# Queueing the preparation of the next token block behind its step's last operations, in a two-layer MoE kernel

## The chip, the cores and the metric

The kernel runs on one core of a Trainium2 chip. Its metric is device time in microseconds; before the change the median of three runs is 1727.81 us (1726.5 to 1728.76). All engines named here belong to the one core: PE (TensorE matmul), PEld (its weight loads), DVE (VectorE), ACT (ScalarE), POOL (GpSimd) and SP (SyncE, which issues the DMAs).

## What is computed

The reference applies two softmax attentions through 32 packed queries, and then two dense layers to the 4608 tokens of width 512. The change lies in the second of them:

```
def _moe2_ref(x, w_gate, w_val, w_out):
    g = x @ w_gate
    silu = g * (1.0 / (1.0 + np.exp(-g)))
    val = x @ w_val
    return (silu * val @ w_out)

# attention (8 x 8 heads x 576 x 64) -> x (4608 x 512)
# x = _moe_ref(x)    d_ff 2048, leaky max
# x = _moe2_ref(x)   d_ff 1536
```

## The kernel before the change

**Layer two.** `NBLK` = 6 blocks s of 768 tokens, each as two halves of 384 columns (`T`). A block takes `NF2` = 12 steps f of 128 hidden columns; step n = 12 s + f is one call of `gv_step` (L1186), and 72 of them follow the 256 units of layer one. A step multiplies the gate and value matrices by seven products (`PRODUCTS`: A11, S2, A12, S3, S1, A22, S4) in place of eight; each of them reads sums of pieces of the token block. One product is six matmuls of 384 columns, since each factor is split into a high and a low part (`mm3`, L302, whose matmuls have the lines L305 to L307). Products 0, 2, 4 and 6 go to one pair of PSUM banks (named xb, and vb for the second of a step), 1, 3 and 5 to the other (yb). Product 2 adds to the bank of product 0, so it can start only when ACT has copied that bank (L1204); product 3 adds to the bank of product 1, so it can start only when DVE has read it in `add(u2, yb, p1)` (an L1184 instruction). Between the products stand the output units of the step before (`out_unit`, tile o), three matmuls of 512 columns each, whose weights are the high and low parts ph and pl that `halves` (L1241) makes on ACT and POOL.

**The order of the work on PE** is written out: each product waits in the queue behind the one before (`behind`, `tc.issue_after`). On DVE, ACT and POOL the instructions of a step stand in the order that a scheduler gives them: it takes what is ready by its own timeline, and earlier program text goes first where two are ready.

**The preparation of a token block** (`prepare_x`, L1124): `load` (DMA of the eight raw tiles xr, L1069), `A11` (high part on ACT, L1120, low part on DVE, L1121, two tiles each), `S` (`sums_x`: L1088 twice on DVE, L1089 twice on POOL), `S2` (L1111 twice on DVE, then L1120 and L1121 twice each), `A12` (L1120, L1121 twice each) and `D4` (`last_sum`, L1095 twice on DVE). The other four splits (S3, S1, A22, S4) are called inside step f = 11 by `next_x` (L1198). `NEXT_X` (L94) names the step of block s in which the program text prepares block s + 1: load 3, A11 and S 6, S2 7, A12 8, D4 9. The split parts lie in a ring of 40 pieces of 384 columns (`fifth`, L1099), of which a block takes 28, so the first three products of the next block have room beside the whole of the present one.

Below, "boundary" means the steps f = 10, 11 and the following f = 0, 1, and "boundary 1 to 2" the one between the blocks 1 and 2.

Of the kernel before, what the change touches and what calls it, by code (L numbers as in the profile page):

```python
# [11 lines left out]
AF = mybir.ActivationFunctionType  # L12
ALU = mybir.AluOpType
# [80 lines left out]
NEXT_X = dict(load=3, A11=6, S=6, S2=7, A12=8, D4=9)  # L94
# [10 lines left out]
def f32(ap):  # L105
    return ap.bitcast(F32)
# [3 lines left out]
def tile_kernel(  # L110
# [23 lines left out]
    nc = tc.nc  # L134
# [671 lines left out]
    for f in range(NF1):  # L806
# [11 lines left out]
        d=quad(3, ["h", "at"]),  # L818
# [64 lines left out]
    for b in range(2, B):  # L883
        d0 = 2 * NB1 * (b - 1)
        steps_of = attention(b)
        for entry in STEPS.split():
            d, names = entry.split(":")
# [172 lines left out]
    def load_x(s):  # L1060
        for t in range(2):
            for c in range(KC):
                raw = utile("u", [P, T], f"xr{s}_{t}{c}")
                raw2[s, t, c] = raw
                a0 = t0 = (2 * s + t) * T
                while t0 < a0 + T:
                    j, c0 = divmod(t0, HS)
                    n = min(HS - c0, a0 + T - t0)
                    nc.sync.dma_start(  # L1069
                        out=raw[:, t0 - a0 : t0 - a0 + n], in_=x1d[j][:, c, c0 : c0 + n]  # L1070
                    )
                    t0 += n
# [6 lines left out]
    def sums_x(s):  # L1079

        if s:
            raw2[s, "S1"] = [utile("x", [P, T], f"xs1_{s}{e}") for e in range(2)]
        else:
            s1 = vp.tile([P, 2, T], F32, tag="v", name="xs1_0")
            raw2[s, "S1"] = [s1[:, e] for e in range(2)]
        for e in range(2):
            a11, a21, a22 = (raws_of(s, n)[e] for n in ("A11", "A21", "A22"))
            nc.vector.tensor_tensor(out=raw2[s, "S1"][e], in0=a21, in1=a22, op=ALU.add)  # L1088
            nc.gpsimd.tensor_tensor(out=a21, in0=a11, in1=a21, op=ALU.subtract)  # L1089

    def last_sum(s):

        for e in range(2):
            a12, s2 = raws_of(s, "A12")[e], raws_of(s, "A11")[e]
            nc.vector.tensor_tensor(out=a12, in0=a12, in1=s2, op=ALU.subtract)  # L1095
# [10 lines left out]
    def split_x(s, name):  # L1106

        if name == "S2":
            src = raws_of(s, "A11")
            for e in range(2):  # L1110
                nc.vector.tensor_tensor(  # L1111
                    out=src[e], in0=raw2[s, "S1"][e], in1=src[e], op=ALU.subtract
                )
        else:
            at = dict(S3="A21", S4="A12").get(name, name)
            src = raw2[s, "S1"] if name == "S1" else raws_of(s, at)
        n = 4 * (len(PRODUCTS) * s + PRODUCTS.index(name))
        x = [[fifth(n + 2 * e + i) for e in range(2)] for i in range(2)]
        for e in range(2):
            nc.scalar.activation(out=x[0][e], in_=src[e], func=AF.Copy)  # L1120
            nc.vector.tensor_tensor(out=x[1][e], in0=src[e], in1=f32(x[0][e]), op=ALU.subtract)  # L1121
        xs2[s, name] = x

    def prepare_x(s, name):  # L1124
        if name == "load":
            load_x(s)
        elif name == "S":
            sums_x(s)
        elif name == "D4":
            last_sum(s)  # L1130
        else:
            split_x(s, name)
# [5 lines left out]
    def load_gv(n):  # L1138
        if n >= NBLK * NF2:
            return  # L1140
        f = n % NF2
        gvw[n] = [
            wpool.tile([P, 7, 2 * P], F32R, tag="C", name=f"gv{n}_{t}", bufs=WBUFS["C"])
            for t in range(2)
        ]
        for t in range(2):
            nc.sync.dma_start(out=f32(gvw[n][t]), in_=wgvd[f][:, t])
# [17 lines left out]
    def product(bank, n, k, start):  # L1165

        s = n // NF2
        x = xs2[s, PRODUCTS[k]]
        hi, lo = gvw[n]
        with behind():  # L1170
            for e in range(2):
                c = slice(e * P, (e + 1) * P)
                last = mm3(
                    bank,
                    (hi[:, k, c], lo[:, k, c]),
                    (x[0][e], x[1][e]),
                    start and e == 0,
                    e == 1,
                    skip_group_check=True,
                )  # L1180
        before[:] = [last]

    def add(out, bank, x):
        nc.vector.tensor_tensor(out=out, in0=bank, in1=x, op=ALU.add)  # L1184

    def gv_step(n, between):  # L1186

        s, f = divmod(n, NF2)  # L1190
        p1, u2, u3, s1, s2 = (
            gp2.tile([P, T], F32, tag=t, name=f"{t}_{n}", bufs=b)
            for t, b in (("p1", 2), ("u2", 2), ("u3", 2), ("s1", 1), ("s2", 1))
        )
        def bank(tag, name):
            return ps.tile([P, 512], F32, tag=tag, name=f"{name}{n}", bufs=2)[:, :T]

        def next_x(name):  # L1198
            if f == NF2 - 1 and s + 1 < NBLK:
                split_x(s + 1, name)  # L1200

        xb, yb = bank("h", "xb"), bank("at", "yb")
        product(xb, n, 0, True)
        nc.scalar.activation(out=p1, in_=xb, func=AF.Copy)  # L1204
        product(yb, n, 1, True)
        add(u2, yb, p1)
        between(0)
        product(xb, n, 2, False)
        nc.scalar.activation(out=s1, in_=xb, func=AF.Sigmoid)
        nc.vector.tensor_tensor(out=s1, in0=xb, in1=s1, op=ALU.mult)  # L1210
        next_x("S3")
        product(yb, n, 3, False)
        add(u3, yb, p1)
        between(1)
        between(2)
        xb = bank("h", "vb")
        product(xb, n, 4, True)
        add(u3, xb, u3)
        next_x("S1")
        product(yb, n, 5, False)  # L1220
        add(p1, yb, p1)
        nc.scalar.activation(out=s2, in_=p1, func=AF.Sigmoid)  # L1222
        nc.gpsimd.tensor_tensor(out=s2, in0=s2, in1=p1, op=ALU.mult)  # L1223
        between(3)
        product(xb, n, 6, False)
        add(u2, xb, u2)
        nc.vector.tensor_tensor(out=s1, in0=s1, in1=u2, op=ALU.mult)  # L1227
        halves(n, 0, s1)
        nc.gpsimd.tensor_tensor(out=s2, in0=s2, in1=u3, op=ALU.mult)
        halves(n, 1, s2)  # L1230
        between(4)
        next_x("A22")
        between(5)
        next_x("S4")
        load_gv(n + 2)
        if s + 1 < NBLK:
            for name, d in NEXT_X.items():
                if f == d:
                    prepare_x(s + 1, name)

    def halves(n, t, x):  # L1241
        hi = utile("a", [P, T], f"ph{n}_{t}", F32R)
        nc.scalar.activation(out=hi, in_=x, func=AF.Copy)  # L1243
        lo = utile("a", [P, T], f"pl{n}_{t}", F32R)
        nc.gpsimd.tensor_tensor(out=lo, in0=x, in1=f32(hi), op=ALU.subtract)  # L1245
        ps2[n, t] = hi, lo
# [70 lines left out]
    for n in range(NBLK * NF2):  # L1317
        gv_step(n, lambda i, n=n: out_next(n, i))
# [39 lines left out]
```

## Time and profile before

| | |
|---|---|
| median of three runs | 1727.81 us (1726.5 to 1728.76) |
| the profiled execution | 1725.98 us, of which the span of the trace is 1723.9 us |
| PE busy | 1623.3 us, 94% of the span |
| PEld / DVE / POOL / ACT busy | 1462.9 / 928.5 / 801.2 / 682.7 us |
| mean granted TensorE clock | 0.973 |
| layer two in the trace | from 860.51 us to the end |

The share of a busy engine is an average over both layers. In layer two PE is busy without a break through most steps, and the breaks stand in a few places; so what counts is the length of single steps, read from the start of the first matmul of a product, and what ended a wait of PE. Matmuls overlap: a matmul's own time (0.33 us) is longer than its distance to the next (0.17 us).

### The profile page before, as it was taken

How to read it: one execution, taken by the hardware profiler on the slowest of the kernel's cores; microseconds unless marked ns; L12 is line 12 of the kernel's file. 1: busy time of each engine (PE TensorE's matmuls, PEld its weight loads, DVE VectorE, ACT ScalarE, POOL GpSimd, SP SyncE). 2: the span in 40 equal slices, each digit the busy share in tenths (PEclk: the TensorE clock that was granted, in tenths of full speed). 3: DMA queues.
4: the chain of work that ended last, by engine and by line, in shares of the span. 5: the costliest groups of instructions: out<-in, count | busy, mean ns of one | idle time of the engine just before them, and what ended most of it. 6: DMA issues, size and time to landing. Idle time of an engine off the chain costs nothing.

```text
span 1723.9 us, 28559 instructions
## 1 busy us (share of the span) xinstructions
PE 1623.3 (94%) x10708; PEld 1462.9 (85%) x10708; DVE 928.5 (54%) x1621; ACT 682.7 (40%) x1511; POOL 801.2 (46%) x824
## 2 busy tenths in 40 slices
PE   6698999999999899999999999989989999999997
PEld 3467798988888789889999989979989998998997
DVE  6988757555756546565653453363364345335332
ACT  5775645555554445554521322232232232223222
POOL 3557744655554555547543343333333343343332
PEclk7799999999999999999999999999999999999999
DMA  9433464636444452543664564455355445444442
GB/s 232 121 101 113 118 160 115 159 108 149 124 123 119 133 151 71 139 143 124 221 247 149 186 197 161 171 183 189 144 187 173 168 179 184 171 169 170 168 171 80
DMA packets 227370, 266.11 MB, mean 154 GB/s; under 512 B 130464, under 2 KB 189856, under 8 KB 227232
## 3 DMA queue, kind: packets, MB, share of 16 engines
q1 hardware_dynamic: 227232, 264.30, 48.8%
q8 instruction: 84, 1.38, 0.3%
q14 instruction: 54, 0.44, 0.1%
HBM read 214.70 MB, written 49.55 MB: 153 GB/s over the span
## 4 chain that ended last, share of the span: by engine, by line
PE 68%; DMA 9%; DVE 8%; issue 5%; POOL 4%; ACT 4%; SPq 2%; POOLq 0%; ACTq 0%; DVEq 0%
PE o L306 5%; PE o L307 5%; PE o L305 5%; PE acc L1029 5%; PE acc L1030 4%; PE acc L1035 4%; PE yb L305 4%; PE yb L307 4%; PE yb L306 4%; DMA wgvd<-cva 4%; PE vb L306 3%; PE vb L307 3%; PE vb L305 3%; PE h L305 3%; PE xb L306 3%
## 5 line engine op out<-in xcount | busy, mean ns | idle before, releaser
L1016 POOL TENSOR_TENSOR lo<-g,hi 128x288 fp32r<-128x288 f32 x256 | 227.3, 889 | 237.7 <-ACT hi L1014 195.1
L1223 POOL TENSOR_TENSOR s<-s,p 128x384 f32<-128x384 f32 x72 | 73.9, 1027 | 463.1 <-ACT s L1222 463.1
L1006 DVE SCALAR_TENSOR_TENSOR g<-h,sg,m 128x288 f32<-128x288 f32 x256 | 130.2, 509 | 162.8 <-ACT m L1003 131.3
L305 PE MATMUL h<-a2h,ppw 128*128 128x288 f32 x512 | 163.0, 318 | 22.7 <-DVE g L1006 16.9
L1184 DVE TENSOR_TENSOR u<-vb,u 128x384 f32<-128x384 f32 x144 | 80.2, 557 | 185.8 <-PE vb L307 185.3
L1014 ACT ACTIVATE hi<-g 128x288 fp32r<-128x288 f32 x256 | 113.1, 442 | 153.1 <-DVE g L1006 146.0
L307 PE MATMUL o<-wp,ph 128*128 128x512 f32 x432 | 172.0, 398 | 0.0
L306 PE MATMUL o<-wp,ph 128*128 128x512 f32 x432 | 171.6, 397 | 0.0
L305 PE MATMUL o<-wp,pl 128*128 128x512 f32 x432 | 168.9, 391 | 1.0 <-POOL pl L1245 1.0
L1245 POOL TENSOR_TENSOR pl<-s,ph 128x384 fp32r<-128x384 f32 x144 | 146.8, 1040 | 29.9 <-ACT ph L1243 29.9
L307 PE MATMUL h<-a2l,ppw 128*128 128x288 f32 x512 | 153.1, 299 | 0.0
L305 PE MATMUL yb<-ring,gv 128*128 128x384 f32 x432 | 146.3, 339 | 7.1 <-DVE u L1184 6.8
L306 PE MATMUL h<-a2h,ppw 128*128 128x288 f32 x512 | 152.8, 298 | 0.0
L1222 ACT ACTIVATE s<-p 128x384 f32<-128x384 f32 x72 | 37.8, 525 | 288.2 <-DVE p L1184 288.2
L1184 DVE TENSOR_TENSOR u<-yb,p 128x384 f32<-128x384 f32 x144 | 79.4, 551 | 130.9 <-PE yb L307 129.5
L305 PEld LDWEIGHTS h<-a2h,ppw 128*128 128x128 f32 x512 | 98.2, 192 | 56.9 <-DVE g L1006 27.1
L307 PE MATMUL yb<-ring,gv 128*128 128x384 f32 x432 | 144.9, 335 | 0.0
L306 PE MATMUL yb<-ring,gv 128*128 128x384 f32 x432 | 144.8, 335 | 0.0
L1003 ACT ACTIVATE m<-h,sal 128x288 f32<-128x288 f32 x256 | 125.5, 492 | 42.1 <-PE h L307 41.0
L1243 ACT ACTIVATE ph<-s 128x384 fp32r<-128x384 f32 x144 | 73.4, 523 | 150.7 <-DVE s L1227 136.4
L305 PE MATMUL xb<-ring,gv 128*128 128x384 f32 x288 | 97.3, 338 | 7.9 <-DVE u L1184 7.7
L307 PEld LDWEIGHTS h<-a2l,ppw 128*128 128x128 f32 x512 | 98.1, 192 | 0.8 <-issue 0.8
(234 smaller groups left out, 4364.9 us busy)
## 6 DMA issues: line engine op xcount, KB each, us to landing
gv<-wgvd SPq DMA_DIRECT2D x144, 896.0 KB, 6.2
wgvd<-cva SPq DMA_DIRECT2D x84, 256.0 KB, 2.5
cva<-in_moe_w_out_dram SPq DMA_DIRECT2D x28, 512.0 KB, 3.8
v<-in_v_dram SPq DMA_DIRECT2D x16, 576.0 KB, 5.2
out_dram<-os SPq DMA_DIRECT2D x12, 768.0 KB, 3.7
cva<-in_moe_w_in_dram SPq DMA_DIRECT2D x16, 512.0 KB, 3.7
kr<-in_k_dram SPq DMA_DIRECT2D x96, 72.0 KB, 2.8
qr<-in_q_dram SPq DMA_DIRECT2D x96, 72.0 KB, 2.5
```

Of the source, the lines that this page charges most:

```text
L305: nc.tensor.matmul(o, wlo, xhi, start=start, stop=False, **kw)
L306: nc.tensor.matmul(o, whi, xhi, start=False, stop=False, **kw)
L307: return nc.tensor.matmul(o, whi, xlo, start=False, stop=stop, **kw)
L1003: begun[it] = nc.scalar.activation(out=m, in_=hp, func=AF.Copy, scale=sal[:, f : f + 1])
L1006: made[it] = nc.vector.scalar_tensor_tensor(out=g32, in0=hp, scalar=sg[:, f : f + 1], in1=m, op0=ALU.mult, op1=ALU.max)
L1014: rounded[n] = nc.scalar.activation(out=hi, in_=x, func=AF.Copy)
L1016: nc.gpsimd.tensor_tensor(out=lo, in0=x, in1=f32(hi), op=ALU.subtract)
L1029: nc.tensor.matmul(acc[dc], lo[:, f % WP, c], ghi, start=start, stop=False)
L1184: nc.vector.tensor_tensor(out=out, in0=bank, in1=x, op=ALU.add)
L1223: nc.gpsimd.tensor_tensor(out=s2, in0=s2, in1=p1, op=ALU.mult)
L1243: nc.scalar.activation(out=hi, in_=x, func=AF.Copy)
L1245: nc.gpsimd.tensor_tensor(out=lo, in0=x, in1=f32(hi), op=ALU.subtract)
```

## The change

The preparation in a step f of `NEXT_X` is queued on DVE, POOL and ACT behind three instructions of the same step: the second sigmoid on ACT (L1222), the product with it on POOL (L1223) and the last `add` on DVE (`add(u2, xb, u2)`). `tc.issue_after(ins)` makes every instruction of its block that runs on `ins`'s engine stand behind `ins` in that engine's queue; no semaphore is added. Loads (SP) get no such edge. `next_x` is as it was.

```diff
     def add(out, bank, x):
-        nc.vector.tensor_tensor(out=out, in0=bank, in1=x, op=ALU.add)
+        return nc.vector.tensor_tensor(out=out, in0=bank, in1=x, op=ALU.add)
...
-        nc.scalar.activation(out=s2, in_=p1, func=AF.Sigmoid)
-        nc.gpsimd.tensor_tensor(out=s2, in0=s2, in1=p1, op=ALU.mult)
+        latest = [nc.scalar.activation(out=s2, in_=p1, func=AF.Sigmoid)]
+        latest.append(nc.gpsimd.tensor_tensor(out=s2, in0=s2, in1=p1, op=ALU.mult))
         between(3)
         product(xb, n, 6, False)
-        add(u2, xb, u2)
+        latest.append(add(u2, xb, u2))
         nc.vector.tensor_tensor(out=s1, in0=s1, in1=u2, op=ALU.mult)
...
         load_gv(n + 2)
+
         if s + 1 < NBLK:
-            for name, d in NEXT_X.items():
-                if f == d:
-                    prepare_x(s + 1, name)
+            with ExitStack() as held:
+                for ins in latest:
+                    held.enter_context(tc.issue_after(ins.ins))
+                for name, d in NEXT_X.items():
+                    if f == d:
+                        prepare_x(s + 1, name)
```

What moves, in the built programs. PE's order stays the same. The first place is DVE's queue at the end of step 23, the last of block 1 (xr_00 to xr_03, xr_10 to xr_13 and xs_30, xs_31 are raw tiles and sums of block 3; u, p, s are the step's own tiles, numbered by the step). Before:

```order
L1088 TENSOR_TENSOR xs_30_13812<-xr_10_13520,xr_12_13526 128x384
L1088 TENSOR_TENSOR xs_31_13813<-xr_11_13523,xr_13_13529 128x384
L1121 TENSOR_TENSOR ring_10369<-xr_02_13514,ring_10369 128x384
L1184 TENSOR_TENSOR u_23_13017<-vb_13065,u_23_13017 128x384
L1121 TENSOR_TENSOR ring_10419<-xr_03_13517,ring_10369 128x384
L1111 TENSOR_TENSOR xr_00_13508<-xs_30_13812,xr_00_13508 128x384
L1227 TENSOR_TENSOR s_23_13019<-s_23_13019,u_23_13017 128x384
L1111 TENSOR_TENSOR xr_01_13511<-xs_31_13813,xr_01_13511 128x384
L1095 TENSOR_TENSOR xr_02_13514<-xr_02_13514,xr_00_13508 128x384
L1121 TENSOR_TENSOR ring_9954<-xr_00_13508,ring_9954 128x384
L1095 TENSOR_TENSOR xr_03_13517<-xr_03_13517,xr_01_13511 128x384
L1184 TENSOR_TENSOR u_24_13125<-yb_13130,p_24_13124 128x384
```

With the change the same stretch, from the `p` add of step 23 to step 24, reads:

```order
L1184 TENSOR_TENSOR p_23_13016<-yb_13022,p_23_13016 128x384
L1184 TENSOR_TENSOR u_23_13017<-vb_13065,u_23_13017 128x384
L1227 TENSOR_TENSOR s_23_13019<-s_23_13019,u_23_13017 128x384
L1184 TENSOR_TENSOR u_24_13125<-yb_13130,p_24_13124 128x384
L1210 TENSOR_TENSOR s_24_13127<-xb_13129,s_24_13127 128x384
```

Twelve DVE instructions of block 3's preparation left this place, and with them six L1120 of ACT and two L1089 of POOL. The boundaries 0 to 1, 2 to 3 and 3 to 4 lose the same twelve, six and two. Boundary 4 to 5 had none, since there is no block 6; its rows stay as they were, and with the change the other four read row for row like it. Of block 1, four L1120 and four L1121 leave the last units of layer one, and eight DVE, two ACT and two POOL instructions leave step 1.

The second place is where they go, here block 3's A11 and S in step 30 (f = 6 of block 2). DVE, as a piece of the difference:

```order
 L1184 TENSOR_TENSOR u_30_13717<-vb_13761,u_30_13717 128x384
+L1121 TENSOR_TENSOR ring_9954<-xr_00_13508,ring_9883 128x384
+L1088 TENSOR_TENSOR xs_30_13812<-xr_10_13520,xr_12_13526 128x384
+L1088 TENSOR_TENSOR xs_31_13813<-xr_11_13523,xr_13_13529 128x384
+L1121 TENSOR_TENSOR ring_9954<-xr_01_13511,ring_9954 128x384
 L1227 TENSOR_TENSOR s_30_13719<-s_30_13719,u_30_13717 128x384
 L1184 TENSOR_TENSOR u_31_13819<-yb_13824,p_31_13818 128x384
```

POOL in the same step, with the change (L1249 is L1245 of the kernel before):

```order
L1223 TENSOR_TENSOR s_30_13720<-s_30_13720,p_30_13716 128x384
L1229 TENSOR_TENSOR s_30_13720<-s_30_13720,u_30_13718 128x384
L1089 TENSOR_TENSOR xr_10_13520<-xr_00_13508,xr_10_13520 128x384
L1089 TENSOR_TENSOR xr_11_13523<-xr_01_13511,xr_11_13523 128x384
L1249 TENSOR_TENSOR pl_0_13791<-s_30_13719,ph_0_13789 128x384
```

Four DVE instructions now stand between the last `add` of the step and L1227, so also ahead of the next step's first `add`, and two of POOL ahead of the low part pl.

The third place is ACT's queue in step 31 (f = 7), where S2 is prepared. With the change:

```order
L1222 ACTIVATE s_31_13822<-p_31_13818 128x384
L1120 ACTIVATE ring_9954<-xr_00_13508 128x384
L1120 ACTIVATE ring_10369<-xr_01_13511 128x384
L1247 ACTIVATE ph_0_13891<-s_31_13821 128x384
L1204 ACTIVATE p_32_13916<-xb_13921 128x384
L1247 ACTIVATE ph_1_13896<-s_31_13822 128x384
```

Before, the two L1120 were not there, and L1204 of the next step stood behind both ph. The steps f = 8 and f = 9 look like it, f = 8 with two L1120 and f = 9 with none; on DVE each of f = 7, 8 and 9 has two instructions more ahead of L1227, and f = 7 two more behind it.

On SP the DMAs of one raw tile pair of the block after next (xr_00 and xr_01, which take the place of the pair that D4 reads last) move from the first step of a block to its steps 9 and 10, in front of the `gv` loads for the next block's first step.

## Rows read from the trace of the kernel before

**Rows 1.** Waits of PE in layer two: us in total, times, longest us.

```profile
PE xb L305 <- DVE u L1184: 7.7, 4, 2.6
PE yb L305 <- DVE u L1184: 6.8, 5, 3.0
```

**Rows 2.** PE's timeline: start us, us; product 0 of steps f = 10 and 2.

```profile
971.81 0.33 PE L305 MATMUL xb<-ring,gv 128*128 128x384 f32 x1
...
1021.57 0.33 PE L305 MATMUL xb<-ring,gv 128*128 128x384 f32 x1
...
1113.62 0.33 PE L305 MATMUL xb<-ring,gv 128*128 128x384 f32 x1
...
1167.52 0.33 PE L305 MATMUL xb<-ring,gv 128*128 128x384 f32 x1
...
1259.57 0.33 PE L305 MATMUL xb<-ring,gv 128*128 128x384 f32 x1
...
1312.91 0.33 PE L305 MATMUL xb<-ring,gv 128*128 128x384 f32 x1
...
1404.96 0.33 PE L305 MATMUL xb<-ring,gv 128*128 128x384 f32 x1
...
1455.20 0.33 PE L305 MATMUL xb<-ring,gv 128*128 128x384 f32 x1
...
1547.25 0.33 PE L305 MATMUL xb<-ring,gv 128*128 128x384 f32 x1
...
1594.71 0.33 PE L305 MATMUL xb<-ring,gv 128*128 128x384 f32 x1
```

**Rows 3.** PE's timeline at boundary 1 to 2: the longest wait (idle, releaser in brackets).

```profile
1146.53 0.69 PE L305 MATMUL yb<-ring,gv 128*128 128x384 f32 x1 [2.96 <-DVE u L1184]
```

**Rows 4.** Stretch behind that wait: us, busy us, granted clock, DMA share, GB/s.

```profile
1147.00:1156.00 9.00, 9.00 (x41) 8.22 (x41) 4.23 (x7) 1.61 (x3) 1.93 (x2) 0.86 0.20 39
```

**Rows 5.** DVE's timeline ahead of that wait, while POOL is busy.

```profile
1139.87 1.37 DVE L1111 TENSOR_TENSOR xr<-xs,xr 128x384 f32<-128x384 f32 x1
1141.16 1.37 DVE L1227 TENSOR_TENSOR s<-s,u 128x384 f32<-128x384 f32 x1
1142.45 0.54 DVE L1111 TENSOR_TENSOR xr<-xs,xr 128x384 f32<-128x384 f32 x1
1142.92 0.55 DVE L1095 TENSOR_TENSOR xr<-xr,xr 128x384 f32<-128x384 f32 x1
```

**Rows 6.** PE's timeline in step 1 of block 0: its wait.

```profile
877.21 0.45 PE L305 MATMUL vb<-ring,gv 128*128 128x384 f32 x1 [0.82 <-DVE u L1184]
```

**Rows 7.** DVE's timeline, end of step 30 and begin of step 31.

```profile
1223.86 0.56 DVE L1184 TENSOR_TENSOR u<-vb,u 128x384 f32<-128x384 f32 x1 [1.20 <-PE vb L307]
1224.45 0.56 DVE L1227 TENSOR_TENSOR s<-s,u 128x384 f32<-128x384 f32 x1
1227.40 0.56 DVE L1184 TENSOR_TENSOR u<-yb,p 128x384 f32<-128x384 f32 x1 [2.40 <-PE yb L307]
```

**Rows 8.** POOL and ACT in the same stretch.

```profile
1224.45 1.44 POOL L1229 TENSOR_TENSOR s<-s,u 128x384 f32<-128x384 f32 x1
1225.84 1.98 POOL L1245 TENSOR_TENSOR pl<-s,ph 128x384 fp32r<-128x384 f32 x2
...
1225.05 0.53 ACT L1243 ACTIVATE ph<-s 128x384 fp32r<-128x384 f32 x1 [1.76 <-DVE s L1227]
```

**Rows 9.** PE in step 31: first matmuls of product 2, product 3, output unit.

```profile
1227.84 0.33 PE L305 MATMUL xb<-ring,gv 128*128 128x384 f32 x1
...
1228.90 0.33 PE L305 MATMUL yb<-ring,gv 128*128 128x384 f32 x1
...
1229.94 0.39 PE L305 MATMUL o<-wp,pl 128*128 128x512 f32 x1
```

**Rows 10.** ACT's timeline at the end of layer one.

```profile
849.17 1.34 ACT L1120 ACTIVATE ring<-xr 128x384 fp32r<-128x384 f32 x3
```

**Rows 11.** SP's own waits from 840 us on: us in total, times, longest us.

```profile
SPq L1147 <- PE vb L307: 655.7, 69, 14.1
```

## The prediction

> **What bounds the kernel now.** The sum below is made against the profiled execution, 1725.98 us, 2.08 us more than its span of 1723.9 us; the median of the three runs, 1727.81 us, stands 1.83 us above it, and what I gain or lose in the profile I take from the median. I read first who makes PE wait in layer two: DVE, nine times, 14.5 us in all, and always with an L1184 `add` that PE needs before it can write to a bank again [rows 1]. Next I ask where. The starts of product 0 at f = 2 and f = 10 [rows 2] cut layer two into quiet stretches and boundaries. From f = 2 to f = 10 all four whole blocks take 92.05 us (1021.57 to 1113.62 and so on), that is 11.506 us a step. A boundary is four steps, f = 10 to f = 2, and without a wait would take 46.03 us. It takes 49.76, 53.90, 53.34, 50.24 and 47.46 us. The excess is 3.73, 7.87, 7.31, 4.21 and 1.43 us, 24.55 us in all. The last of the five is the boundary at which nothing of a block after next is prepared, and that makes it the control.
>
> Why do the others cost more? At boundary 1 to 2 the longest wait, 2.96 us, ends with `add(u2, yb, p1)` [rows 3], and behind it the granted clock is 0.86 [rows 4], so part of the next 9 us ran at 1.2 in place of 2.4 GHz. Ahead of it, DVE works through preparation and step in one queue, and some of its 128x384 instructions take 1.37 us in place of 0.55 [rows 5]. The pattern is regular: while POOL is busy too, starts follow each other every 1.29 us (1139.87, 1141.16, 1142.45), and at once every 0.47 us where POOL pauses (1142.45, 1142.92). DVE instructions with two SBUF inputs and POOL instructions take turns.
>
> **What goes.** At four boundaries twelve DVE, six ACT and two POOL instructions leave, and the remaining order on all three engines is that of the control. So I price each of the four at the control's excess: 3.73 + 7.87 + 7.31 + 4.21 - 4 x 1.43 = **17.4 us** gained. What stays late there is the control's own: the four splits of `next_x` and the output copies. The control has no loads of new raw tiles on SP, and the four have them; the `gv` loads queued behind them wait for the last product of an earlier step anyhow, 69 times and 655.7 us in all [rows 11], so a load ahead of them that waits only for the splits of f = 11 or D4 of f = 9 ends first. I cost it at nothing; were that cover gone, a late `gv` tile would stop PE's first product directly.
>
> In block 0, PE waits 0.82 us in step 1, again for such an `add` [rows 6], behind the twelve instructions of block 1's preparation there, which leave too. The start of that matmul is late by the 0.82 us and by 0.16 us more, since a matmul's own 0.33 us reach over the next one's start 0.17 us later; with 0.1 us for the restart (it takes 0.45 in place of 0.33 us) I count **1.1 us** gained, bounds 0.8 and 1.1.
>
> At the end of layer one, four L1120 and four L1121 of block 1 leave, but the order of the rest also shifts: three L1120 of block 0, 1.34 us together [rows 10], now stand ahead of a scaling copy (L1003) that they followed. It frees the PSUM bank of one unit of layer one later by that time at most. The bounds are a loss of 1.3 us and, as four ACT and four DVE instructions leave, a gain of the same size; I take **0.5 us** lost, nearer to none, since a single unit is hit.
>
> **What is added.** The same preparation now stands at f = 6 to 9 of the blocks 0 to 4, five times four steps. PE waits there for nothing today. Step 30 is such an f = 6 [rows 7 to 9]. Its last `add` ends at 1224.42; L1227 starts at 1224.45; the next step's first `add` can start at 1227.40, when its bank is full, and ends at 1227.96; PE's product 3, which needs it, starts at 1228.90. So that `add` has 0.9 us to spare, and DVE is idle for 2.40 us before it.
>
> At f = 6 four DVE instructions come ahead of L1227, five in a row with it, while POOL has three: L1229 and two L1089. Free of POOL they would end by 1224.45 + 4 x 0.47 + 0.56 = 1226.9, before 1227.40, and cost nothing. If all five paid the turn of 1.29 us, they would end at 1230.9, and the `add` at 1231.4, 2.5 us after product 3's start. POOL has three instructions in that stretch, so three of the five can pay: 3 x 1.29 + 2 x 0.47 = 4.81, end 1229.3, `add` done by 1229.8, product 3 late by 0.9 us. The high part ph follows L1227 (0.53 us) and its low part takes 1.0 us on POOL [rows 8]: 1229.3 + 1.5 = 1230.8, which is when the output unit (1229.94) would start after that delay. With 0.1 us for the restart and 0.1 us for that unit I take 1.1 us, bounds 0 and 2.5.
>
> This is where the Trainium skill can be weighed. The page "Advanced Engine Details and Errata", section "VectorE Performance Modes", says that GpSimd and VectorE's two-port instructions block each other, and names no other. By it these fp32 additions of two tensors would not wait, and the sum would be 5.5 us better. The rows of 1.37 us speak against it [rows 5]; the page "SBUF — State Buffer", section "Who interferes with whom", has the rule that agrees with them, that two SBUF inputs are enough.
>
> At f = 7, 8 and 9 two DVE instructions come ahead of L1227 and only L1229 stands beside them: 0.47 + 1.29 = 1.76 us, so L1227 ends at 1226.8, ph at 1227.3, and L1204, now behind ph on ACT, at 1227.8. PE's product 2 starts at 1227.84. That is just in time; I take 0.1 us each, bounds 0 and 0.7 (both paying the turn and a restart). Per block 1.1 + 0.3 = 1.4 us, over five blocks **7.0 us**; bounds 0 and 5 x (2.5 + 2.1) = 23 us.
>
> **Sum.** 17.4 + 1.1 - 0.5 - 7.0 = 11.0 us gained: the profiled execution would go to 1715.0 us, the median to 1727.81 - 11.0 = **1716.8 us**.
>
> **The rivals.**
> 1. The turns cost nothing at f = 6 to 9, because DVE gets through before POOL's three instructions: 18.0 us gained, 1709.8 us. For it: DVE's 2.40 us of idle time. Against: L1229 already starts within 0.03 us of L1227 and takes 1.44 us there [rows 7, 8].
> 2. The gain is given back: 3.6 us per block (18.0 / 5), 1727.8 us. For it: DVE can be 2.5 us late at f = 6 alone. Against: only three POOL instructions are there.
> 3. Slower: DVE loses the turn to POOL for every instruction of f = 6 to 9. Each block then pays 4.6 us, 23.0 us in all, 5.0 us more than the gain: 1732.8 us. It decides from 3.6 us per block. Against it stands that L1229 is the one POOL instruction in three of the four steps.
> 4. The change does not clear the boundaries: raw tiles that now arrive later, or the `next_x` splits, hold them as long as before for half the excess. Then 8.7 us of the 17.4 stay: 2.3 us gained, 1725.5 us. For it: the loads of the first raw pair move. Against: the control, and that the pair is needed twelve steps later.
>
> **How the numbers follow.** A measurement of this kernel can tell 0.2%, 3.5 us, from no change: below 1724.4 us is faster, above 1731.3 us slower. My forecast has a chance of 0.74, the free turns 0.10, the gain given back 0.06, the boundaries that stay 0.04, the slower case 0.06. Faster: 0.74 + 0.10 = 0.84; same: 0.06 + 0.04 = 0.10; slower: 0.06. The range begins where the additions and the end of layer one cost nothing, 1727.8 - 18.5 = 1709.3 us (layer one's possible gain left out), and ends where f = 6 stands at its upper bound and the rest as taken, 5 x 2.8 = 14.0 us in place of 7.0, 1723.8 us. Half of rival 1 and nearly all of the forecast lie in it.
>
> **What would show it.** In the profile after, product 0 from f = 10 to f = 2 takes about 47.5 us at all five boundaries, with no wait of 1 us or more and the clock at full speed behind it; if they stay above 50 us, the first step is wrong. Step 1 of block 0 has no wait. PE waits for an L1184 in five steps f = 7, each product 3 about 0.9 us late; from f = 2 to f = 10 a block takes 93.4 us in place of 92.05. If that stretch takes over 95.6 us, the additions have eaten the gain. POOL's L1089 and DVE's L1121 of f = 6 show 1.3 us where they alternate. The orders on PE and the number of instructions are the same, so a changed busy time of PE beyond its waits would speak for the clock.

## The result and the profile after

| | before | after |
|---|---|---|
| median | 1726.5 us (1717.67 to 1728.76, 5 runs) | 1708.84 us (1702.25 to 1711.16, 5 runs) |
| the profiled execution | 1725.98 us | 1711.16 us |
| layer two in the trace | 863.38 us, from 860.51 us | 845.78 us, from 863.58 us |

The ratio after to before is 0.9899 (95% interval 0.988 to 0.9918): 17.4 us less, 14.2 to 20.7. The interval excludes 1, so the kernel is faster, as forecast, but by half as much again as the 11.0 us of the forecast, and its time lies 0.46 us below the low end of the range (1709.3 us). That margin is smaller than the move of the reference: with two more runs the median before went from 1727.81 us, on which the range was built, to 1726.5 us. In gains the range goes from 4.0 to 18.5 us; 17.4 us lies inside it, near its upper end, and the 18.97 us from 1727.81 us lie outside.

The two profiled executions lie 14.8 us apart, less than the medians, because layer one took 3.07 us longer in the one after; 2.44 us of that are there already at 792 us, ahead of the first instruction that the change moves. The starts of layer two in the nine traces of this study lie between 858.5 and 863.8 us, those of the kernel before at 860.51 and 860.26 us and those of the changed kernel at 863.58 and 858.54 us. So the terms are read in layer two, by the starts of product 0. There the change brought 17.60 us.

The busy times after (the profile's first part):

```profile
PE 1614.0 (94%) x10708; PEld 1458.3 (85%) x10708; DVE 923.8 (54%) x1621; ACT 683.4 (40%) x1511; POOL 804.6 (47%) x824
```

The same instructions as before; PE's busy time is down by 9.3 us without a single matmul less. Part of that is the clock, below. The waits of PE in layer two, which answer to [rows 1] (us in total, times, longest us):

```profile
PE yb L305 <- DVE u L1184: 3.4, 5, 0.7
```

Nine waits of 14.5 us have become five of 3.4 us, each at the step f = 7 that the forecast named. Product 0 at f = 10 and f = 2, PE's timeline after, the first two boundaries and the last (answers to [rows 2]):

```profile
974.86 0.33 PE L305 MATMUL xb<-ring,gv 128*128 128x384 f32 x1
...
1021.33 0.33 PE L305 MATMUL xb<-ring,gv 128*128 128x384 f32 x1
...
1114.46 0.33 PE L305 MATMUL xb<-ring,gv 128*128 128x384 f32 x1
...
1161.09 0.33 PE L305 MATMUL xb<-ring,gv 128*128 128x384 f32 x1
...
1533.53 0.33 PE L305 MATMUL xb<-ring,gv 128*128 128x384 f32 x1
...
1580.14 0.33 PE L305 MATMUL xb<-ring,gv 128*128 128x384 f32 x1
```

The boundaries take 46.47, 46.63, 46.47, 46.61 and 46.61 us, against 46.03 us without a wait: 2.64 us of excess in place of 24.54. The control, the last of them, fell too, from 47.46 to 46.61 us, though nothing was taken from it. The stretch f = 2 to f = 10 grew from 92.05 to 93.13 us (1021.33 to 1114.46). Behind the place of the wait of [rows 3] the clock is now full (PE's, PEld's, DVE's, ACT's and POOL's busy us, then the granted clock, DMA share, GB/s; answers to [rows 4]):

```profile
1146.00:1155.00 9.00, 9.00 (x48) 8.33 (x47) 2.79 (x5) 2.94 (x6) 4.40 (x4) 1.00 0.70 207
```

Where the preparation now stands, step 30 on DVE (answers to [rows 5, 7]):

```profile
1217.43 0.56 DVE L1184 TENSOR_TENSOR u<-vb,u 128x384 f32<-128x384 f32 x1 [1.20 <-PE vb L307]
1217.91 0.55 DVE L1121 TENSOR_TENSOR ring<-xr,ring 128x384 fp32r<-128x384 f32 x1
1218.38 1.84 DVE L1088 TENSOR_TENSOR xs<-xr,xr 128x384 f32<-128x384 f32 x2
1220.14 1.36 DVE L1121 TENSOR_TENSOR ring<-xr,ring 128x384 fp32r<-128x384 f32 x1
1221.42 1.37 DVE L1227 TENSOR_TENSOR s<-s,u 128x384 f32<-128x384 f32 x1
1222.72 0.54 DVE L1184 TENSOR_TENSOR u<-yb,p 128x384 f32<-128x384 f32 x1
```

and on POOL (answers to [rows 8]):

```profile
1218.03 1.30 POOL L1229 TENSOR_TENSOR s<-s,u 128x384 f32<-128x384 f32 x1
1219.82 2.56 POOL L1089 TENSOR_TENSOR xr<-xr,xr 128x384 f32<-128x384 f32 x2 [0.49 <-DVE xs L1088]
```

Of DVE's five instructions ahead of the step's next `add`, three take a turn of about 1.3 us (one of the two L1088, an L1121, L1227) and two go at 0.5 us: POOL has three instructions there and no more. The `add` ends at 1223.26 us, and PE's product 3 follows at once, late by 0.85 us (answers to [rows 9]):

```profile
1223.32 0.44 PE L305 MATMUL yb<-ring,gv 128*128 128x384 f32 x1 [0.68 <-DVE u L1184]
```

At the end of layer one, ACT (answers to [rows 10]) has the scaling copy L1003 behind three L1120:

```profile
851.08 1.34 ACT L1120 ACTIVATE ring<-xr 128x384 fp32r<-128x384 f32 x3
852.32 0.48 ACT L1003 ACTIVATE m<-h,sal 128x288 f32<-128x288 f32 x1
```

and PE a gap there that before did not have:

```profile
853.89 0.40 PE L305 MATMUL h<-a2h,ppw 128*128 128x288 f32 x1 [0.48 <-DVE g L1006]
```

Since matmuls overlap, the gap costs more than its 0.48 us: from the fifth `h` matmul of the unit before (849.10 us before, 851.39 us after) to layer two pass 11.41 us before and 12.19 us after, 0.78 us more.

In step 1 of block 0 the wait of [rows 6] is gone, and the step takes 10.82 us in place of 11.94. SP's waits ahead of the `gv` loads (answers to [rows 11]) show no new bound:

```profile
SPq L1147 <- PE vb L307: 672.2, 70, 12.1
```

### The profile page after: what moved, and what is told of

Same layout as the page of the kernel before. It is cut to its first block, busy times and chain, and to the rows that moved or that the text cites. A ratio compares the mean times of both kernels' runs of the same rounds, so it can differ in the third digit from the quotient of the medians.

```text
span 1709.4 us, 28545 instructions
## 1 busy us (share of the span) xinstructions
PE 1614.0 (94%) x10708; PEld 1458.3 (85%) x10708; DVE 923.8 (54%) x1621; ACT 683.4 (40%) x1511; POOL 804.6 (47%) x824
## 4 chain that ended last, share of the span: by engine, by line
PE 70%; DVE 8%; DMA 6%; POOL 5%; issue 5%; ACT 4%; SPq 2%; DVEq 0%; POOLq 0%; ACTq 0%
PE o L306 6%; PE o L307 6%; PE o L305 6%; PE acc L1029 5%; PE yb L305 4%; PE acc L1035 4%; PE acc L1030 4%; PE yb L307 4%; PE yb L306 4%; PE vb L306 3%; PE vb L307 3%; PE vb L305 3%; PE xb L306 3%; PE xb L307 3%; PE xb L305 3%
## 5 line engine op out<-in xcount | busy, mean ns | idle before, releaser
L1223 POOL TENSOR_TENSOR s<-s,p 128x384 f32<-128x384 f32 x72 | 73.2, 1016 | 468.7 <-ACT s L1222 468.7
L1249 POOL TENSOR_TENSOR pl<-s,ph 128x384 fp32r<-128x384 f32 x144 | 145.4, 1031 | 32.3 <-ACT ph L1247 32.3
L1222 ACT ACTIVATE s<-p 128x384 f32<-128x384 f32 x72 | 37.9, 526 | 301.8 <-DVE p L1184 301.8
L1003 ACT ACTIVATE m<-h,sal 128x288 f32<-128x288 f32 x256 | 125.6, 492 | 44.0 <-PE h L307 43.0
L1229 POOL TENSOR_TENSOR s<-s,u 128x384 f32<-128x384 f32 x72 | 98.9, 1373 | 5.6
L1210 DVE TENSOR_TENSOR s<-xb,s 128x384 f32<-128x384 f32 x72 | 40.1, 557 | 110.0 <-ACT s L1209 110.0
```

Source lines behind the costliest of these rows:

```text
L1003: begun[it] = nc.scalar.activation(out=m, in_=hp, func=AF.Copy, scale=sal[:, f : f + 1])
```

## The experiments

All ratios are to the kernel before, run on the same chip. E1 to E4 shared one chip (before: 1729.21 us, 15 runs), E5 to E7 another (1726.2 us, 9 runs).

**E1: the kernel before, a second profile.** No edit. The question: is the control's 1.43 us the price of a boundary that prepares nothing, or one lost turn?

> The kernel before, unchanged, a second profile. The question is the price of the control, boundary 4 to 5: 47.46 us from f = 10 to f = 2 in the first profile, 46.6 us (excess 0.4 to 0.6) at all five boundaries of the kernel after, though the order of the queues is the same. Theory 'lost turn': in the first profile L1227 of step 58 took 1.43 us, since POOL's L1229 got in first; where L1227 shows 0.56 us at f = 10, step 59 takes 11.8 us, and where it shows 1.43 us, 12.5 us. Rival 'fixed price': step 59 takes 12.47 us again whatever L1227 shows. The other four boundaries take 49.5 to 54 us again by both, 23 to 25 us of excess in all five.

Measured: 1724.47 us, one run. The control boundary took 46.58 us, an excess of 0.55 us; its step f = 11 took 11.86 us in place of 12.47. DVE at the control in the first profile of the kernel before:

```profile
1558.16 1.43 DVE L1227 TENSOR_TENSOR s<-s,u 128x384 f32<-128x384 f32 x1
1560.59 2.35 DVE L1121 TENSOR_TENSOR ring<-xr,ring 128x384 fp32r<-128x384 f32 x2 [1.01 <-ACT ring L1120]
1562.86 0.55 DVE L1184 TENSOR_TENSOR u<-yb,p 128x384 f32<-128x384 f32 x1
```

and in this second one:

```profile
1556.94 0.56 DVE L1227 TENSOR_TENSOR s<-s,u 128x384 f32<-128x384 f32 x1
1558.64 2.42 DVE L1121 TENSOR_TENSOR ring<-xr,ring 128x384 fp32r<-128x384 f32 x2 [1.15 <-ACT ring L1120]
1560.99 0.55 DVE L1184 TENSOR_TENSOR u<-yb,p 128x384 f32<-128x384 f32 x1
```

From the start of L1227 to the start of the `add` pass 4.70 us in the first and 4.05 us in the second. In the first, POOL's L1229 started with L1227 and ran 1.02 us, and L1227 took 1.43; in the second it was L1229 that took 1.44. The fixed price falls, the lost turn holds: step f = 11 makes 0.61 us of the 0.88 us between the two controls, and step f = 1 nearly all of the rest (11.97 and 11.71 us). In the seven other profiles (after, E2 to E7) L1227 took 0.56 us at the control, and the control's excess lies between 0.38 and 0.75 us. So the first profile is the only one of nine with the lost turn there. The other four boundaries took 50.81, 52.17, 51.83 and 51.35 us; their sum with the control, 22.59 us of excess, is near the first profile's 24.54 and 0.4 us below the 23 to 25 us expected.

**E2: only DVE's part of the change.**

```diff
-        latest = [nc.scalar.activation(out=s2, in_=p1, func=AF.Sigmoid)]
-        latest.append(nc.gpsimd.tensor_tensor(out=s2, in0=s2, in1=p1, op=ALU.mult))
+        nc.scalar.activation(out=s2, in_=p1, func=AF.Sigmoid)
+        nc.gpsimd.tensor_tensor(out=s2, in0=s2, in1=p1, op=ALU.mult)
...
-        latest.append(add(u2, xb, u2))
+        latest = [add(u2, xb, u2)]
```

> The change with its edge on DVE alone (behind the last add); ACT and POOL are not held. By the order, DVE then has the same instructions at f = 11 as the kernel after (six L1121), while ACT has ten L1120 there in place of six. Theory 'DVE's queue makes the boundary': the boundaries stay near those after, 46.4 to 47.5 us, and the time within 0.3% of the kernel after. Rival 'ACT's queue does, by the high parts that come ahead of its copies': the boundaries go back at least half way, over 48.5 us, and 6 us or more of the gain are gone.

Measured: 1709.19 us (1706.39 to 1711.99, 4 runs), ratio 0.988 (0.9852 to 0.9908). Layer two takes 844.59 us, the boundaries 4.46 us of excess; 1.3 us of it belong to one step, where an output copy on DVE (L1273) waited for its DMA. The stretches f = 2 to f = 10 take 92.5 us in place of the 93.1 us after the change. The part on DVE alone gives what the whole change gives, and the four more L1120 that ACT keeps at each of the four boundaries cost nothing that shows.

**E3: only the parts on ACT and POOL.**

```diff
-        latest.append(add(u2, xb, u2))
+        add(u2, xb, u2)
```

> The change with its edges on ACT and POOL alone; DVE is not held. By the order, DVE then has two L1088 more at f = 11 than after, in front of raw tiles that have only just come. Theory 'DVE's queue': these two cost at each of the four boundaries a wait for the tiles and two turns, 1 to 3 us, boundaries 47.5 to 49.5 us, and the gain over before is 5 to 10 us smaller than that of the kernel after; L1088 shows a wait on a DMA. Rival 'ACT's queue': boundaries as after, below 47 us.

Measured: 1726.82 us (1721.28 to 1729.9, 10 runs), ratio 0.9983 (0.9967 to 0.9998). Nearly the whole gain is gone, some 15 us, more than the 5 to 10 us expected. Layer two takes 861.39 us, 15.6 us more than after the change. 8.9 us of that are boundaries (11.53 us of excess against 2.64), and 6.7 us the five stretches f = 2 to f = 10 (94.46 us each against 93.13), which was not expected. Of the boundaries' part some 1.5 us are a fall of the clock behind one wait (step 12 took 13.15 us, steps 24, 36 and 48 11.62 to 11.64 us). DVE's timeline at boundary 0 to 1:

```profile
997.81 1.34 DVE L1088 TENSOR_TENSOR xs<-xr,xr 128x384 f32<-128x384 f32 x1 [0.78 <-DMA xr<-x1d]
...
1000.44 0.56 DVE L1088 TENSOR_TENSOR xs<-xr,xr 128x384 f32<-128x384 f32 x1 [1.29 <-DMA xr<-x1d]
1000.92 0.55 DVE L1184 TENSOR_TENSOR u<-vb,u 128x384 f32<-128x384 f32 x1
```

The `add` for which PE waits stands behind sums for a block that is due twelve steps later, and these wait for raw tiles. PE, right after:

```profile
1001.52 0.44 PE L305 MATMUL xb<-ring,gv 128*128 128x384 f32 x1 [1.94 <-DVE u L1184]
```

Two of DVE's waits in layer two (us in total, times, longest):

```profile
DVE ring L1121 <- ACT ring L1120: 21.7, 20, 1.1
...
DVE xs L1088 <- DMA xr<-x1d: 6.1, 7, 1.3
```

The second is what the boundaries pay in part; before, the same group came to 4.3 us in 6 waits, and after the change there is none. The first was 5.5 us in 5 waits before and 5.7 us in 5 after the change, all at f = 11; here fifteen more stand at f = 6, 7 and 8, 1.07 us each. The high part (L1120) is held back on ACT, the low part (L1121), which needs it, is not held on DVE, and so it waits at the head of DVE's queue, ahead of the step's last `add`. Against the kernel before, this half brings 13.0 us at the boundaries and costs 12.0 us in the stretches. The other half, E2, has no such wait at f = 6 to 9: there the low part is held and the high part is not.

**E4: POOL's part behind the low part pl instead of behind the product L1223.** At f = 6 POOL's two L1089 then leave the stretch in which DVE has its five instructions. `halves` returns its last POOL instruction:

```diff
-        halves(n, 1, s2)
+        latest.append(halves(n, 1, s2))
...
+        return last_lo
```

> The kernel after, with POOL's two L1089 of f = 6 queued behind the step's last pl (L1249) in place of behind L1223. DVE's order is that of the kernel after, four instructions ahead of L1227. Theory 'turns': the step f = 7 is 1.1 us too long after the change because three of DVE's five instructions wait for one of POOL's; with L1229 alone beside them it is one, 4 x 0.47 + 1.29 = 3.2 us, the next add ends 0.8 us before product 3 needs it, and the step takes 11.5 us: 92.05 us from f = 2 to f = 10 in place of 93.1, and 5 to 5.5 us less in all than the kernel after. Rival 'four instructions in the queue': the number on DVE's queue counts, not POOL, and f = 7 stays at 12.6 us and the time at that of the kernel after.

Measured: 1705.35 us (1703.6 to 1711.88, 5 runs), ratio 0.9866 (0.9842 to 0.989). The stretch f = 2 to f = 10 is back at 92.03 us, and step f = 7 at 11.51. DVE's timeline in step 30:

```profile
1213.33 0.55 DVE L1121 TENSOR_TENSOR ring<-xr,ring 128x384 fp32r<-128x384 f32 x1
1213.79 1.84 DVE L1088 TENSOR_TENSOR xs<-xr,xr 128x384 f32<-128x384 f32 x2
1215.55 0.55 DVE L1121 TENSOR_TENSOR ring<-xr,ring 128x384 fp32r<-128x384 f32 x1
1216.02 0.55 DVE L1227 TENSOR_TENSOR s<-s,u 128x384 f32<-128x384 f32 x1
1216.49 0.55 DVE L1184 TENSOR_TENSOR u<-yb,p 128x384 f32<-128x384 f32 x1
```

and POOL's:

```profile
1213.44 1.30 POOL L1229 TENSOR_TENSOR s<-s,u 128x384 f32<-128x384 f32 x1
1217.21 1.99 POOL L1249 TENSOR_TENSOR pl<-s,ph 128x384 fp32r<-128x384 f32 x2 [2.46 <-ACT ph L1247]
1219.15 2.00 POOL L1089 TENSOR_TENSOR xr<-xr,xr 128x384 f32<-128x384 f32 x2
```

The orders of DVE and ACT are those after the change; only POOL's two instructions have gone, from 1219.82 us there to behind pl here, and with them the two long instructions: L1121 takes 0.55 us in place of 1.36, L1227 0.55 in place of 1.37. One turn, with L1229, is left. So the 1.08 us of each block are DVE's turns with POOL, not DVE's own work. The new place costs nothing that shows in layer two (841.06 us, 4.72 us less than after the change, where 5 to 5.5 us were expected; 5 x 1.10 us come from the stretches, 0.8 us are lost at the boundaries). The intervals of the two ratios overlap (0.9842 to 0.989 here, 0.988 to 0.9918 for the change), so it is the traces that tell the two kernels apart.

**E5: E4, and the splits of S3 at f = 11 behind the step's first `add`.** At f = 11 two L1121 still stood ahead of `add(u2, yb, p1)`, and the step took 11.81 to 11.85 us at all five boundaries.

```diff
-        add(u2, yb, p1)
+        second = add(u2, yb, p1)
...
-        next_x("S3")
+        with tc.issue_after(second.ins):
+            next_x("S3")
```

> The kernel of e4 (POOL's L1089 behind the last pl) with one more edge: the split of S3 in step f = 11 is queued on DVE behind the step's first add (u2 out of yb). In the kernels after and e4 its two L1121 stand ahead of that add at f = 11, and step 11 takes 11.83 us in place of 11.51. Theory 'turns': these two are what makes the add late; behind it, step 11 takes 11.5 us at all five boundaries, 1.6 us in all less than e4, and 6.3 to 7 us less than the kernel after. Rival 'the rest of f = 11': six more L1121 and ACT's six L1120 make it late by themselves, and step 11 stays at 11.8 us or more.

Measured: 1701.94 us (1698.53 to 1708.52, 5 runs), ratio 0.9867 (0.984 to 0.9894). DVE's timeline at f = 11 in E4:

```profile
1122.38 2.42 DVE L1121 TENSOR_TENSOR ring<-xr,ring 128x384 fp32r<-128x384 f32 x2 [1.15 <-ACT ring L1120]
1124.72 0.55 DVE L1184 TENSOR_TENSOR u<-yb,p 128x384 f32<-128x384 f32 x1
```

and in E5:

```profile
1122.79 0.56 DVE L1184 TENSOR_TENSOR u<-yb,p 128x384 f32<-128x384 f32 x1 [2.40 <-ACT p L1204]
1123.27 1.01 DVE L1121 TENSOR_TENSOR ring<-xr,ring 128x384 fp32r<-128x384 f32 x2
```

Step f = 11 fell to 11.58 to 11.60 us (11.5 expected), and the excess of the boundaries from 3.45 to 1.98 us. In layer two that is 839.69 us, 1.37 us less than E4. The ratios of E4 and E5 cannot tell that apart. E5 has the lowest median of all kernels run.

**E6: E4 with the preparation back at the boundary, at f = 0 to 3 (d in `NEXT_X`).** Is it the position in the step that matters, or the step?

```diff
-NEXT_X = dict(load=3, A11=6, S=6, S2=7, A12=8, D4=9)
+NEXT_X = dict(load=0, A11=0, S=0, S2=1, A12=2, D4=3)
```

> The kernel of e4 with the preparation at f = 0 to 3 in place of 6 to 9 (load 0, A11 and S 0, S2 1, A12 2, D4 3), still behind the step's last operations. The question is whether the boundaries got short because the preparation left them, or because it stands behind the step's last add, wherever that is. Theory 'position in the step': f = 0 and 1 take at most 1 us more than in e4 (the output copies share these steps), f = 11 stays at 11.8 us, and the time is within 0.3% of e4. Rival 'distance from the boundary': raw tiles that have only just landed and the output copies make DVE wait again, f = 0 and 1 together take 25 us or more in place of 23.3, and 5 us or more are lost in all.

Measured: 1706.51 us (1703.15 to 1709.36, 4 runs), ratio 0.9886 (0.9865 to 0.9908). Layer two takes 844.08 us, 3.02 us more than E4. 1.93 us of that are step 1 of block 0, 12.73 us in place of 10.80. As at every f = 0, the preparation behind the last `add` of step 0 stands ahead of the first `add` of step 1. But step 0 of block 0 is short (7.32 us, without output units of a step before), and there DVE has little time ahead of that `add`. In E4, without the preparation, it idles 0.51 us, where it idled 2.40 us in step 31 [rows 7]:

```profile
870.58 0.56 DVE L1184 TENSOR_TENSOR u<-yb,p 128x384 f32<-128x384 f32 x1 [0.51 <-PE yb L307]
```

Of the other steps f = 1, those of blocks 1 and 3 took 12.35 and 12.87 us (E4: 11.84 and 11.97), and the longer of them reads, on DVE:

```profile
1294.43 0.69 DVE L1274 COPY os<-o 128x512 f32<-128x512 f32 x1 [2.17 <-DMA out_dram<-os]
1295.04 0.55 DVE L1184 TENSOR_TENSOR u<-yb,p 128x384 f32<-128x384 f32 x1
```

That is an output copy which waits for the DMA out of its buffer, as in E2; no preparation stands between it and the `add` before it. All steps f = 0 of the blocks 1 to 4 took 11.51 us. So at the start of a block, f = 0 to 3, twelve preparing instructions on DVE cost next to nothing, as long as they stand behind the `add`s of their step and DVE idles long enough ahead of the next one. Position explains most; the short step 0 of block 0 is the exception. That the load at f = 0 makes the output DMA later is possible and was not tried.

**E7: the changed kernel, a second profile.** No edit.

> The kernel after, unchanged, on the same chip as e5 and e6, for its time beside theirs and a second profile. Expected of the profile: f = 7 of the blocks 0 to 4 at 12.6 us, boundaries 46.4 to 46.9 us, and layer two from product 0 of step 0 to the end within 1 us of 845.8 us.

Measured: 1709.11 us (1706.47 to 1711.13, 4 runs), ratio 0.9901 (0.9882 to 0.992). Boundaries 46.59, 46.56, 46.58, 46.62 and 46.69 us, stretches 93.17 us, layer two 846.15 us from 858.54 us on: the reading above repeats. On this chip E5's median is 7.2 us lower and its layer two 6.5 us shorter; the interval of its ratio overlaps this one's by 0.0012 only.

## Why the prediction was right in its sign and short in its size

By the terms of its sum, from the profiles before and after (layer two by product 0, layer one by the stretch that holds the gap):

| term | forecast | measured |
|---|---|---|
| four boundaries that lose the preparation | 17.4 us | 21.06 us |
| the control boundary | 0 | 0.85 us |
| step 1 of block 0 | 1.1 us | 1.12 us |
| end of layer one | -0.5 us | -0.78 us |
| additions at f = 6 to 9 | -7.0 us | -5.4 us |
| sum | 11.0 us | 16.85 us |

The measured sum agrees with the 17.4 us (14.2 to 20.7) of the ratio. By the second profile of the kernel before (E1), the four boundaries give 20.0 us and the control nothing.

- **The step that failed** is "I price each of the four at the control's excess: 3.73 + 7.87 + 7.31 + 4.21 - 4 x 1.43". The mechanism was right, since the four did become what the control is; but the control's 1.43 us was not a constant. E1 shows the same kernel with 0.55 us there, once L1227 wins the turn; the changed kernel has 0.58 and 0.66 us at the control, and 0.44 to 0.60 us at the four, which take 46.5 to 46.6 us in place of the 47.5 us forecast. With 0.5 us as the price the term is 23.12 - 2.0 = 21.1 us. This term makes 3.7 us of the 5.85 us by which the sum fell short; the additions make 1.6 us and the control 0.85 us. That the one profile had the lost turn at the control was bad luck, one case of nine.
- **The range** had no bound for that price. One boundary of five was the only instance, it contained an L1227 that had lost its turn, a length that the rows on turns [rows 5] showed to depend on POOL, and while the other terms had bounds, this one had none. Bounds of 0 and 1.43 us would have added 4 x 1.43 = 5.7 us at the low end: 1703.6 us.
- **f = 6** was right in its number: 3 x 1.29 + 2 x 0.47 for the five instructions, product 3 late by 0.9 us (0.85 measured), 1.1 us per block (1.10 at f = 7). E4 shows the cause by taking it away. By the Trainium skill's page "SBUF — State Buffer", section "Who interferes with whom", a DVE instruction with two SBUF inputs contends with a GpSimd instruction that reads SBUF. The trace agrees: 0.55 us without POOL beside it, 1.36 and 1.37 us with it. The Trainium skill's page "Advanced Engine Details and Errata", section "VectorE Performance Modes", names two-port instructions alone; were they the only ones hit, step f = 7 would have stayed at 11.51 us, and it took 12.61.
- **f = 7, 8 and 9** cost nothing where I took 0.1 us each: their following steps took 11.49 or 11.51 us. "Just in time" was in time. This is the 1.6 us between -7.0 and -5.4.
- **Step 1** came out as worked out. **The end of layer one** lost 0.78 us by the very copy that the forecast named: in E2, where ACT is not held, the gap is missing and the stretch takes 11.43 us. Its size in the forecast was a choice inside bounds of 1.3 us either way, so that it came near is in part luck.
- **The rivals.** Free turns (1709.8 us) lies near the time measured, but for a wrong reason: the turns at f = 6 cost 5.4 us, and the five boundaries gave 4.5 us more than forecast. Gain given back and slower fall with 1.1 us per block, against 3.6 and 4.6. Boundaries that stay by half falls with 46.5 us; E3 shows what that case looks like, 11.53 us of excess and stretches of 94.46 us, when the queue of DVE is left out of the change.
- **The clock** was counted into the boundaries without a price of its own. The last section gives it: steps with a fall are 0.84 to 1.55 us longer than the same steps without.

Open: L1227 took its long form of 1.42 us or more in 23 and 26 of 72 steps in the two profiles of the kernel before, in 4 and 8 in those of the changed one, in none in E4, in 8 and 10 in E5 and E6. Most of these lie in steps with time to spare and cost nothing. Why the changed kernels lose that turn less often was not found.

## What to carry to other kernels

Work for later that shares an in-order queue with work that is due now belongs behind the step's last due instruction, first of all on the engine for which the critical one waits. Here that was DVE: held alone it gave the whole gain (E2). With the others held and DVE not, its parts waited at the head of their queue for the parts held, and the gain was gone (E3). Between DVE and POOL it was here the number of POOL instructions beside a run of two-input DVE instructions that set its length, so move POOL's too (E4). And a control taken from a single instance is a sample: give it bounds, or a second profile of the same kernel, before it prices four others.

## What the runs showed of the hardware that was not expected

**The same wait, with and without a fall of the clock.** In the second profile of the kernel before (E1), PE waited as in the first, 2.98 us in place of 2.96 at boundary 2 to 3:

```profile
1290.85 0.44 PE L305 MATMUL yb<-ring,gv 128*128 128x384 f32 x1 [2.98 <-DVE u L1184]
```

The stretch behind it there (the granted clock stands ahead of the DMA share):

```profile
1291.00:1300.00 9.00, 9.00 (x47) 8.33 (x48) 5.08 (x8) 2.13 (x5) 2.03 (x2) 1.00 0.31 62
```

and the stretch behind the wait of 2.96 us in the first profile:

```profile
1292.00:1301.00 9.00, 9.00 (x39) 8.09 (x39) 4.06 (x8) 1.61 (x3) 1.49 (x2) 0.81 0.16 35
```

At 0.81 the engine ran part of these 9 us at 1.2 GHz, at 1.00 all of them at 2.4. Steps 24 and 36, which hold this wait and the one of [rows 3], took 16.50 and 16.66 us in the first profile and 15.11 us each in the second, with waits of the same length. In the second profile the clock fell at the two other boundaries, 0 to 1 and 3 to 4, behind shorter waits of 2.48 and 2.77 us; the stretch behind the first of them:

```profile
998.00:1007.00 9.00, 9.00 (x42) 8.44 (x41) 7.91 (x13) 3.34 (x7) 3.86 (x3) 0.81 0.39 131
```

In the first profile it stayed at 1.00 there, behind waits of 2.25 and 2.63 us, and steps 12 and 48 took 12.35 us in place of 13.19. In E3 it fell behind the wait of 1.94 us:

```profile
1002.00:1011.00 9.00, 9.00 (x41) 8.44 (x40) 2.65 (x6) 2.41 (x5) 1.97 (x2) 0.81 0.27 108
```

The length of one wait thus did not decide by itself; what did, these traces do not show. The changed kernel, whose waits in layer two's boundaries are gone, had 1.00 in both profiles through all steps of layer two but the last.

**Who comes first.** DVE's L1227 and POOL's L1229 are often released together. The one that loses took 1.43 us or so, and which one it is differs between executions of the same program, as at the control in E1.
